# Third buffers for a transform's input and its two halves, and the last software DMAs moved to other queues

## The chip, the cores and the metric

One core of one Trainium2 chip runs the whole program. The metric is the device time in microseconds (us) of one execution. The engines are TensorE (PE, with its weight loads as PEld), VectorE (DVE), ScalarE (ACT), GpSimd (POOL) and SyncE (SP). SP, ACT and POOL also issue DMA transfers; each of these engines takes its instructions and its DMA issues strictly in order, so that an issue that waits holds up everything behind it on that engine.

## The reference

```python
# x: (8, 3072, 256); weights come as float64
X = np.fft.rfft(x, axis=1)
x = np.fft.irfft(X * (filt_r + 1j * filt_i), n=3072, axis=1)      # per channel
x_prev = shift x by one position
xk = mu_k * x + (1 - mu_k) * x_prev
xr = mu_r * x + (1 - mu_r) * x_prev
k = max(xk @ w_k, 0)                                              # 256 -> 1024
x = sigmoid(xr @ w_r) * (k * k @ w_v)                             # 1024 -> 256
h = max(x @ w1, x @ w2, x @ w3)                                   # 256 -> 768
out = h @ w_out                                                   # 768 -> 256
```

## The kernel before

**The transform.** 3072 = 48 x 64, and each batch is transformed by matmuls in two stages. The a-stage (16 steps) loads `xa`, splits it into a rounded high part `xah` and the remainder `xal`, multiplies by the resident table `wa_s` into `pa`, copies that to `ao` and stores it to DRAM (`s1`). The b-stage (12 steps) loads a 512 KB table `wbc`, a filter `filt` and `xb`, splits `xb`, multiplies (`pb`), applies the filter on DVE and POOL, splits the result into `yh` and `yl`, multiplies back (`pc`), copies to `co` and stores to DRAM (`s2`). A product of two values costs three matmuls (`mm3`): high x high, high x low, low x high.

**The rest.** `y_load` brings 384 KB of `s2` into `cin`, `y_mm` finishes the inverse transform (`py`), mixes with the previous position (`xm`) and splits (`xh`, `xl`). `kv(i)` (64 chunks of 384 positions) does the three products with w_k, w_v, w_r (`pk`, `pv`, `pr`). `combos` and `second(p)` do the 768-wide layers for a pair of chunks, in nine blocks of seven products (`pb`, `pa`, `pe`) with combined weights streamed from DRAM into the `ws` tiles; `o_mm` does the last product.

**Weights.** They arrive as float64. `narrow` makes float32 of a piece: one ACT operation into `we` (L212), five DVE operations (L213, L214, L215 on `we`, L218, L219 on `wm`) and one POOL addition into `wf` (L222); the parts are then a copy on ACT (L229) or DVE (L231) and a subtraction on POOL (L232). Pieces 0 to 8 (w_k, w_v, w_r) run beside the transform of the first batch; the twelve others (nine of w1, w2, w3 and three of w_out) are put among the units of the first chunks.

**Buffers.** The pool `fp` has two buffers for each tag, unless a line says otherwise. Tag `fin` holds `xa`, `xb` and `wm`; tags `flo` and `fhi` hold `xal`, `xbl`, `yl` and `xah`, `xbh`, `yh` and, in turn, `wf`; tag `fo` holds `we`, `ao` and `co`.

**What sets the order.** The first batch's transform (`fft_first`) is plain float32 and has its order on SP, ACT and PE written by hand; its filter step on DVE is L547, and its product `q` on POOL is L544. Everything else is ordered by a scheduler with a timing model of its own, which sees the units in the order of the list `units`; the transform of batch b + 1 is interleaved with the units of batch b by `drive`, except that nothing of it stands in the first `lead` units of batch 0.

**Software DMAs.** Three kinds of transfer are issued by POOL and go by the software queue: `wa_s` (which casts on the way), the four stores `wvd` of the prepared w_v (L273), and, in the second batch's transform only, the twelve `wbc` tables (L367, casting), each of which ACT then stores to DRAM (`wbcd`, L369) for the later batches to read.

Of the kernel before, what the change touches and what calls it, by code (L numbers as in the profile page):

```python
# [94 lines left out]
def as_float(bits):  # L95
    return float(np.uint32(bits).view(np.float32))
# [29 lines left out]
def tile_spectral_moe(ctx: ExitStack, tc, x, filt, ones, wa, wa1, wi, wbc, wb1, wc1, filt1, filt0, mu, w_k, w_v, w_r, w1, w2, w3, w_out, out):  # L126
    nc = tc.nc
    B = x.shape[0]
    P = 128
    C = 256  # L130
# [33 lines left out]


    wa_s = cpool.tile([NP, 2, NQ], F32R, name="wa_s")
    nc.gpsimd.dma_start(wa_s, wa)
    wi_s = cpool.tile([NQ, 2, NP], F32, name="wi_s")
    mu_s = cpool.tile([P, 2, 2], F32, name="mu_s")
    nmu_s = cpool.tile([P, 2, 2], F32, name="nmu_s")  # L170

    def load_small():
        nc.scalar.dma_start(wi_s, wi)
        nc.scalar.dma_start(mu_s, mu)
        nc.vector.tensor_scalar(nmu_s, mu_s, -1.0, 1.0, op0=ALU.mult, op1=ALU.add)

# [5 lines left out]
    cnt = [0]  # L182

    def piece(src, kt, t0, t1, c0, c1, parts):

        wide = src.dtype != F32
        if wide:
            src = src.bitcast(I32)
        v = src.rearrange("(t p) n -> p t n", p=P)
        a, c = t1 - t0, c1 - c0  # L190
        st = {}

        def load(stage=None):
            if stage is not None:
                st["t"] = stage.rearrange("p (a n) -> p a n", a=a)
            elif wide:
                st["t"] = fp.tile([P, a, 2 * c], I32, tag="filt", name="wst", bufs=3)
            else:
                st["t"] = fp.tile([P, a, c], F32, tag="filt", name="wst", bufs=3)
            k = 2 if wide else 1  # L200
            nc.sync.dma_start(st["t"], v[:, t0:t1, k * c0 : k * c1])

        def narrow(late=True):
            if not wide:
                st["r"] = st["t"]
                return
            w = st["t"].rearrange("p a (n k) -> p a n k", k=2)
            low, high = w[:, :, :, 0], w[:, :, :, 1]

            e = fp.tile([P, a, c], I32, tag="fo", name="we")  # L210
            ef = e.bitcast(F32)
            nc.scalar.activation(ef, high.bitcast(F32), AF.Abs)  # L212
            nc.vector.tensor_scalar(ef, ef, as_float(0x38000000), as_float(0x47EFFFFF), op0=ALU.max, op1=ALU.min)  # L213
            nc.vector.tensor_scalar(e, e, 3, 0x3FFFFFFF, op0=ALU.logical_shift_left, op1=ALU.bitwise_and)  # L214
            nc.vector.scalar_tensor_tensor(e, high, -0x40000000, e, ALU.bitwise_and, ALU.bitwise_or)  # L215
            m = fp.tile([P, a, c], I32, tag="fin", name="wm")
            mf = m.bitcast(F32)
            nc.vector.tensor_scalar(m, e, -0x800000, None, op0=ALU.bitwise_and)  # L218
            nc.vector.scalar_tensor_tensor(mf, low.bitcast(U32), 2.0**-52, mf, ALU.mult, ALU.mult)  # L219
            cnt[0] += 1  # L220
            r = fp.tile([P, a, c], F32, tag=("flo", "fhi")[cnt[0] % 2], name="wf")
            nc.gpsimd.tensor_tensor(r, ef, mf, ALU.add)  # L222
            st["r"] = r

        return load, narrow, lambda late=True: parts(st["r"], late)

    def to_parts(hi, lo, r, late):
# [23 lines left out]
    wv_d = [dp.tile([P, 2, 2, C], F32, tag=f"wvd{q}", name=f"wvd{q}", bufs=1) for q in range(NF // 2)]  # L251
# [17 lines left out]
    def wv_job(q):  # L269
        def parts(r, late):  # L270
            t = fp.tile([P, 2, 2, C], F32R, tag="wbc", name="wvs", bufs=3)
            to_parts(t[:, :, 0], t[:, :, 1], r, late)
            nc.gpsimd.dma_start(wv_d[q], t.bitcast(F32))  # L273

        return piece(w_v, NF, 2 * q, 2 * q + 2, 0, C, parts)

# [45 lines left out]
    wjobs2 = pipelined([wu_job(k) for k in range(NB)] + wo[2])  # L322


    s2_of = {}
    wbc_d = {}

    def fft(b):

# [5 lines left out]
        pieces = []  # L335

        def a_load(s):
            t = fp.tile([NP, 2, C], F32, tag="fin", name="xa")
            nc.sync.dma_start(t, xv[:, 2 * s : 2 * s + 2, :])
            hi = fp.tile([NP, 2, C], F32R, tag="fhi", name="xah")  # L340
            lo = fp.tile([NP, 2, C], F32R, tag="flo", name="xal")
            split(hi, lo, t, nc.gpsimd)
            st["a", s] = hi, lo

# [17 lines left out]

        def b_load(s):
            w = fp.tile([NK, 4, 2, NK], F32R, tag="wbc", name="wbc", bufs=3)
            if b == 1:

                nc.gpsimd.dma_start(w, wbc[:, s])  # L367
                wbc_d[s] = dp.tile([NK, 4, 2, NK], F32, tag=f"wbcd{s}", name=f"wbcd{s}", bufs=1)
                nc.scalar.dma_start(wbc_d[s], w.bitcast(F32))  # L369
            else:  # L370
                nc.sync.dma_start(w.bitcast(F32), wbc_d[s])
            f = fp.tile([NK, 2, 2, C], F32, tag="filt", name="filt", bufs=3)
            nc.sync.dma_start(f, filt[:, s])
            t = fp.tile([NK, 2, C], F32, tag="fin", name="xb")
            nc.sync.dma_start(t, s1.rearrange("m r g c -> (m r) g c")[:, 2 * s : 2 * s + 2, :])
            hi = fp.tile([NK, 2, C], F32R, tag="fhi", name="xbh")
            lo = fp.tile([NK, 2, C], F32R, tag="flo", name="xbl")
            split(hi, lo, t)
            st["b", s] = w, f, hi, lo

        def b_mm(s):
            w, f, hi, lo = st.pop(("b", s))
            p = ps.tile([NK, 2, C], F32, tag="pm", name="pb")
            for g in range(2):
                mm3(p[:, g], [(w[:, 0, g], w[:, 1, g])], [(hi[:, g], lo[:, g])], g > 0, True)

            fr, fi = f[:, 0], f[:, 1]
            H = NK // 2
            nc.vector.scalar_tensor_tensor(fi[:H], p[H:], -1.0, fi[:H], ALU.mult, ALU.mult)
            nc.vector.tensor_tensor(fi[H:], p[:H], fi[H:], ALU.mult)  # L390
            nc.vector.tensor_tensor(fr, p, fr, ALU.mult)
            (nc.gpsimd).tensor_tensor(fr, fr, fi, ALU.add)
            yh = fp.tile([NK, 2, C], F32R, tag="fhi", name="yh")
            yl = fp.tile([NK, 2, C], F32R, tag="flo", name="yl")
            split(yh, yl, fr)
            st["c", s] = w, yh, yl

# [477 lines left out]
    units = kv(0) + kv(1) + kv(2) + [(0.0, lambda: combos(0))] + kv(3)  # L875
    marks, cuts = {}, {}
    before2 = len(units)
    s, left = second(0)
    units += s
    units.append((0.0, lambda: combos(1)))  # L880
    for p in range(1, NPAIR):
# [5 lines left out]
        s, left = second(p)  # L887
# [11 lines left out]

    for k, fn in enumerate(wjobs2):  # L900
        units.insert(min(3 + int(k * (before2 - 3) / (NB + 1.5)), before2 + 10 + 3 * (k - NB)) + k, (0.0, fn))
    n2 = len(wjobs2)

    lead = before2 + n2
    starts = [0] + [marks[b] + n2 for b in range(1, B)]
# [62 lines left out]
```

## Time and profile before

| | |
|---|---|
| median of 3 runs | 3200.22 us (3198.54 to 3203.57) |
| the profiled execution | 3198.21 us, span 3196.4 us |
| mean granted clock of TensorE | 0.991 |
| busy: PE, ACT, POOL, DVE | 97%, 60%, 58%, 56% |
| DMA | 676.38 MB moved, of which 8.46 MB by the software queue |

A busy share is a mean over the whole span. With PE at 97% the question is where the other 3% stand and what PE waits for there, so the stretches are read one by one: the start up to 120 us, the conversion of the weights up to the first `second` at about 225 us, the second batch's transform, and the long steady part behind 480 us.

### The profile page before, as it was taken

What the parts mean: (1) busy time and instruction counts of PE and PEld (TensorE: products, weight loads), DVE (VectorE), ACT (ScalarE), POOL (GpSimd) and SP (SyncE); (2) the same over time, 40 slices, a digit from 0 to 9 for tenths busy, and PEclk for the clock granted to TensorE, in tenths of its full rate; (3) what the DMA queues carried; (4) which work ended last, traced back from release to release, by engine and by line L of the source; (5) the groups of instructions that cost most, each with busy time, mean ns of one, the idle gap of its engine ahead of it and who ended that gap; (6) DMA issues with size and microseconds to landing.
All of it is one profiled execution on the core that took longest, in us unless ns stands there. A gap on an engine that the chain in (4) does not pass through costs nothing.

```text
span 3196.4 us, 55749 instructions
## 1 busy us (share of the span) xinstructions
PE 3105.7 (97%) x19256; PEld 3031.7 (95%) x19256; DVE 1784.9 (56%) x2882; ACT 1913.8 (60%) x4024; POOL 1864.1 (58%) x1619
## 2 busy tenths in 40 slices
PE   6799999999999999999999999999999999999998
PEld 4789999999999999999999999999999999999998
DVE  4865564456554665456645466446664456555554
ACT  5556556656666566656666566665666566655554
POOL 3545675567655676546666566566665567544443
PEclk9899999999999999999999999999999999999999
DMA  8767796657766676757766577665876667555553
GB/s 292 234 227 226 235 329 192 195 181 247 246 197 184 213 241 211 215 173 234 257 198 186 178 259 252 198 191 165 269 249 189 190 195 245 182 170 160 166 168 122
DMA packets 397783, 676.38 MB, mean 212 GB/s; under 512 B 41920, under 2 KB 153664, under 8 KB 396864
## 3 DMA queue, kind: packets, MB, share of 16 engines
q1 hardware_dynamic: 328336, 585.61, 58.4%
q10 hardware_dynamic: 66752, 78.75, 7.2%
q0 software_dynamic: 2416, 8.46, 0.8%
q8 instruction: 156, 2.56, 0.3%
q14 instruction: 123, 1.01, 0.1%
HBM read 580.51 MB, written 92.14 MB: 210 GB/s over the span
## 4 chain that ended last, share of the span: by engine, by line
PE 84%; DMA 6%; DVE 5%; issue 2%; ACT 2%; POOL 1%; ACTq 0%; SPq 0%; POOLq 0%; DVEq 0%
PE pb L153 19%; PE pk L153 14%; PE pv L153 14%; PE po L153 12%; PE pe L153 9%; PE pa L153 7%; PE pr L153 4%; PE py L153 3%; DMA ws<-wud 3%; PE pc L153 2%; DVE xm L607 1%; DMA xb<-s 1%; PE ps L153 1%; DVE sc L665 1%; DVE m L748 1%
## 5 line engine op out<-in xcount | busy, mean ns | idle before, releaser
L153 PE MATMUL pb<-x,ws 128*128 128x384 f32 x3456 | 753.1, 338 | 23.0 <-DMA ws<-wud 16.9
L179 POOL TENSOR_TENSOR hh<-m,hh 128x384 fp32r<-128x384 f32 x384 | 402.2, 1056 | 522.4 <-ACT hh L178 426.3
L179 POOL TENSOR_TENSOR klo<-kr,khi 128x384 fp32r<-128x384 f32 x492 | 515.8, 1058 | 231.6 <-ACT khi L178 218.7
L153 PEld LDWEIGHTS pb<-x,ws 128*128 128x128 f32 x3456 | 598.7, 188 | 39.0 <-issue 15.2
L633 DVE SCALAR_TENSOR_TENSOR kr<-pk,kr 128x384 f32<-128x384 f32 x512 | 280.7, 553 | 444.9 <-ACT kr L632 443.6
L153 PE MATMUL po<-wo_hi,hh 128*128 128x256 f32 x2304 | 481.0, 283 | 3.1 <-ACT hh L178 1.6
L153 PE MATMUL pv<-khi,ws 128*128 128x384 f32 x2048 | 474.6, 337 | 4.0 <-ACT khi L178 4.0
L153 PEld LDWEIGHTS po<-wo_hi,hh 128*128 128x128 f32 x2304 | 389.9, 190 | 7.6 <-ACT hh L178 4.0
L153 PE MATMUL pe<-x,ws 128*128 128x384 f32 x1728 | 389.0, 337 | 0.6
L178 ACT CAST khi<-kr 128x384 fp32r<-128x384 f32 x512 | 260.2, 513 | 185.0 <-DVE kr L633 167.6
L153 PEld LDWEIGHTS pv<-khi,ws 128*128 128x128 f32 x2048 | 360.4, 188 | 7.0 <-ACT khi L178 5.3
L153 PE MATMUL pk<-xh,wk_hi 128*128 128x384 f32 x1024 | 341.4, 338 | 7.6 <-ACT xh L178 6.2
L153 PE MATMUL pk<-xl,wk_hi 128*128 128x384 f32 x1024 | 343.6, 336 | 0.9 <-DVE xl L179 0.9
L153 PE MATMUL pk<-xh,wk_lo 128*128 128x384 f32 x1024 | 343.4, 335 | 0.0
L153 PE MATMUL po<-wo_lo,hh 128*128 128x256 f32 x1152 | 316.6, 282 | 0.0
L632 ACT ACTIVATE kr<-pk 128x384 f32<-128x384 f32 x512 | 249.9, 490 | 109.0 <-POOL klo L179 48.7
L748 DVE TENSOR_TENSOR m<-sc,m 128x384 f32<-128x384 f32 x384 | 307.8, 806 | 9.2
L153 PEld LDWEIGHTS pe<-x,ws 128*128 128x128 f32 x1728 | 296.0, 188 | 3.1 <-PE pb L153 2.2
L153 PE MATMUL pv<-klo,ws 128*128 128x384 f32 x1024 | 292.3, 337 | 0.8 <-POOL klo L179 0.4
L179 POOL TENSOR_TENSOR xl<-xm,xh 128x768 fp32r<-128x768 f32 x126 | 233.4, 1869 | 89.7 <-ACT xh L178 89.7
L178 ACT CAST hh<-m 128x384 fp32r<-128x384 f32 x384 | 193.0, 514 | 134.2 <-DVE m L748 67.0
L607 DVE SCALAR_TENSOR_TENSOR xm<-yt,nmu_s,xm 128x384 f32<-128x384 f32 x256 | 180.1, 748 | 145.4 <-ACT xm L606 145.4
(129 smaller groups left out, 6028.0 us busy)
## 6 DMA issues: line engine op xcount, KB each, us to landing
ws<-wud SPq DMA_DIRECT2D x864, 256.0 KB, 3.5
ws<-wvd SPq DMA_DIRECT2D x512, 256.0 KB, 3.3
filt<-in_filt SPq DMA_DIRECT2D x84, 512.0 KB, 5.3
ws<-wud SPq DMA_DIRECT2D x288, 128.0 KB, 3.5
wbc<-wbcd SPq DMA_DIRECT2D x72, 512.0 KB, 5.4
cin<-s SPq DMA_DIRECT2D x64, 384.0 KB, 4.2
out_dram<-osb ACTq DMA_DIRECT2D x192, 128.0 KB, 3.1
xb<-s SPq DMA_DIRECT2D x85, 256.0 KB, 3.5
```

The costliest lines, as they stand in the source:

```text
L153: nc.tensor.matmul(o, lhsT=wgt, rhs=rhs, start=start, stop=stop, skip_group_check=more)
L178: nc.scalar.copy(hi, src)
L179: (lo_eng or nc.gpsimd).tensor_tensor(lo, src, hi.bitcast(F32), ALU.subtract)
L607: nc.vector.scalar_tensor_tensor(v[:, h], yt[:, h, :, :MC], nmu_s[:, w, h : h + 1], v[:, h], ALU.mult, ALU.add)
L632: nc.scalar.activation(r, p, AF.Relu)
L633: nc.vector.scalar_tensor_tensor(r, p, 0.0, r, ALU.max, ALU.mult)
L665: eng.tensor_tensor(t, a, b, ALU.subtract)
L748: nc.vector.tensor_tensor(m, c, m, ALU.max)
```

## The change

- Tags `fin`, `flo` and `fhi` get a third buffer, in room taken from the software queue's scratch (4096 to 1024).
- `wa_s` is loaded by ACT's queue into a float32 tile of tag `fin` and copied by DVE.
- The four `wvd` stores are issued by ACT.
- The `wbc` tables are rounded ahead of the second batch's transform, in 24 units `short(s, n)` of half a table each: SP loads 256 KB into `wbf` (tag `fin`), ACT copies it into `wbr` (tag `fo`, which keeps two buffers), SP stores it to `wbcd`. The units stand at places 24, 28, ... 116 of the list, inside the lead. The second batch then reads its twelve tables from `wbcd` on SP, as the later ones do.

```diff
     wa_s = cpool.tile([NP, 2, NQ], F32R, name="wa_s")
-    nc.gpsimd.dma_start(wa_s, wa)
...
     def load_small():
         nc.scalar.dma_start(wi_s, wi)
+        t = fp.tile([NP, 2, NQ], F32, tag="fin", name="wa_t", bufs=3)
+        nc.scalar.dma_start(t, wa)
+        nc.vector.tensor_copy(wa_s, t)
...
-            m = fp.tile([P, a, c], I32, tag="fin", name="wm")
+            m = fp.tile([P, a, c], I32, tag="fin", name="wm", bufs=3)
...
-            r = fp.tile([P, a, c], F32, tag=("flo", "fhi")[cnt[0] % 2], name="wf")
+            r = fp.tile([P, a, c], F32, tag=("flo", "fhi")[cnt[0] % 2], name="wf", bufs=3)
...
-            nc.gpsimd.dma_start(wv_d[q], t.bitcast(F32))
+            nc.scalar.dma_start(wv_d[q], t.bitcast(F32))
...
-    wbc_d = {}
+    wbc_d = [dp.tile([NK, 4, 2, NK], F32, tag=f"wbcd{s}", name=f"wbcd{s}", bufs=1) for s in range(NG // 2)]
+
+    def short(s, n):
+        t = fp.tile([NK, 2, 2, NK], F32, tag="fin", name="wbf", bufs=3)
+        tc.keep_in_program_order(nc.sync.dma_start(t, wbc[:, s, n : n + 2]))
+        r = fp.tile([NK, 2, 2, NK], F32R, tag="fo", name="wbr")
+        nc.scalar.copy(r, t)
+        nc.sync.dma_start(wbc_d[s][:, n : n + 2], r.bitcast(F32))
...
-            t = fp.tile([NP, 2, C], F32, tag="fin", name="xa")
+            t = fp.tile([NP, 2, C], F32, tag="fin", name="xa", bufs=3)
...
-            hi = fp.tile([NP, 2, C], F32R, tag="fhi", name="xah")
-            lo = fp.tile([NP, 2, C], F32R, tag="flo", name="xal")
+            hi = fp.tile([NP, 2, C], F32R, tag="fhi", name="xah", bufs=3)
+            lo = fp.tile([NP, 2, C], F32R, tag="flo", name="xal", bufs=3)
...
-            if b == 1:
-
-                nc.gpsimd.dma_start(w, wbc[:, s])
-                wbc_d[s] = dp.tile([NK, 4, 2, NK], F32, tag=f"wbcd{s}", name=f"wbcd{s}", bufs=1)
-                nc.scalar.dma_start(wbc_d[s], w.bitcast(F32))
-            else:
-                nc.sync.dma_start(w.bitcast(F32), wbc_d[s])
+            nc.sync.dma_start(w.bitcast(F32), wbc_d[s])
...
     for k, fn in enumerate(wjobs2):
         units.insert(min(3 + int(k * (before2 - 3) / (NB + 1.5)), before2 + 10 + 3 * (k - NB)) + k, (0.0, fn))
-    n2 = len(wjobs2)
+    for k in range(NG):
+        units.insert(24 + 4 * k, (0.0, lambda k=k: short(k // 2, k % 2 * 2)))
+    n2 = len(wjobs2) + NG
...
-    nc = _bacc.Bacc("TRN2", target_bir_lowering=False, num_devices=1, dynamic_dma_scratch_size=4096)
+    nc = _bacc.Bacc("TRN2", target_bir_lowering=False, num_devices=1, dynamic_dma_scratch_size=1024)
```

`xb`, `xbh`, `xbl`, `yh` and `yl` get `bufs=3` in the same way. The changed kernel's own line numbers are a few higher: L550 there is L547 here, L213 to L222 become L215 to L224, and L178 becomes L180.

Where the change moves instructions, the compiled orders show it. The first place is DVE at the end of the first batch's transform. A number behind a name counts tiles; L547 (L550 after the change) is the filter step of the transform, the other rows convert pieces 6 and 7 of the weights. Before, the last L547 stood here:

```order
L215 SCALAR_TENSOR_TENSOR we_625<-wst_471,we_625 128x512 [waits DMAHW3_49,DVE_49]
L547 SCALAR_TENSOR_TENSOR filt1_418<-pb_509,sgn_119,filt1_418 128x512 [waits DMAHW1_49,PE_49,Pool_49]
L218 TENSOR_SCALAR wm_630<-we_625 128x512 [waits DVE_49]
L219 SCALAR_TENSOR_TENSOR wm_630<-wst_471,wm_630 128x512 [waits DVE_49]
L213 TENSOR_SCALAR we_639<-we_639 128x512 [waits Activation_49,Pool_49]
L214 TENSOR_SCALAR we_639<-we_639 128x512 [waits DVE_49]
L215 SCALAR_TENSOR_TENSOR we_639<-wst_507,we_639 128x512 [waits DMAHW4_49,DVE_49]
L213 TENSOR_SCALAR we_653<-we_653 128x512 [waits Activation_49,Pool_49]
L218 TENSOR_SCALAR wm_644<-we_639 128x512 [waits DVE_49]
L214 TENSOR_SCALAR we_653<-we_653 128x512 [waits DVE_49]
L219 SCALAR_TENSOR_TENSOR wm_644<-wst_507,wm_644 128x512 [waits DVE_49]
L215 SCALAR_TENSOR_TENSOR we_653<-wst_568,we_653 128x512 [waits DMAHW7_49,DVE_49]
```

In the changed kernel the same place on DVE reads:

```order
L550 SCALAR_TENSOR_TENSOR filt1_377<-pb_487,sgn_130,filt1_377 128x512 [waits PE_49,Pool_49]
L216 TENSOR_SCALAR we_653<-we_653 128x512 [waits DVE_49]
L215 TENSOR_SCALAR we_667<-we_667 128x512 [waits Activation_49]
L217 SCALAR_TENSOR_TENSOR we_653<-wst_521,we_653 128x512 [waits DMAHW5_49,DVE_49]
L216 TENSOR_SCALAR we_667<-we_667 128x512 [waits DVE_49]
L220 TENSOR_SCALAR wm_658<-we_653 128x512 [waits DVE_49]
L217 SCALAR_TENSOR_TENSOR we_667<-wst_582,we_667 128x512 [waits DMAHW0_49,DVE_49]
L550 SCALAR_TENSOR_TENSOR filt1_408<-pb_504,sgn_130,filt1_408 128x512 [waits PE_49,Pool_49]
L221 SCALAR_TENSOR_TENSOR wm_658<-wst_521,wm_658 128x512 [waits DVE_49]
L220 TENSOR_SCALAR wm_672<-we_667 128x512 [waits DVE_49]
L550 SCALAR_TENSOR_TENSOR filt1_432<-pb_523,sgn_130,filt1_432 128x512 [waits DMAHW2_49,PE_49,Pool_49]
L221 SCALAR_TENSOR_TENSOR wm_672<-wst_582,wm_672 128x512 [waits DVE_49]
```

Of the twelve conversion operations that stood behind the transform's last filter step (ten are L213 to L219 of the last two pieces, two belong to the piece ahead), one still stands behind it; the other eleven have moved ahead of it.

The second place is ACT where the first two blocks of `second` end and the second batch's a-stage begins. In the changed kernel ACT has the following there (`v` is the last copy that the first two blocks need; `wbr` the copies of `short`; `we` and `wo_hi` belong to the last weights; `xah` is the first high part of the second batch):

```order
L704 COPY v_2168<-pb1_2129 128x384 [waits PE_49]
L231 CAST wo_hi_90<-wf_1892 128x512 [waits Pool_49]
L334 CAST wbr_1920<-wbf_1918 128x512 [waits DMAHW5_49,DVE_49]
L334 CAST wbr_1955<-wbf_1953 128x512 [waits DMAHW6_49,DMAHW1_49,Activation_49]
L334 CAST wbr_1996<-wbf_1994 128x512 [waits DMAHW3_49,DMAHW2_49,Activation_49]
L214 ACTIVATE we_2009<-wst_1882 128x512 [waits DMAHW4_49,Activation_49]
L334 CAST wbr_2053<-wbf_2051 128x512 [waits DMAHW6_49,DMAHW5_49,Activation_49]
L334 CAST wbr_2076<-wbf_2074 128x512 [waits DMAHW7_49,Pool_49]
L231 CAST wo_hi_90<-wf_2017 128x512
L334 CAST wbr_2101<-wbf_2099 128x512 [waits DMAHW2_49,DMAHW1_49,Activation_49]
L214 ACTIVATE we_2104<-wst_2007 128x512 [waits DMAHW3_49,Activation_49]
L180 CAST xah_2123<-xa_2121 96x512 [waits DMAHW5_49]
```

Before, none of the `wbr` copies existed, and `xah` stood among the copies of the last chunk ahead of `second`. SP carries the stores of these copies and the load of `xa` in the same queue, in this order after the change:

```order
L335 DMA wbcd9_101<-wbr_1920 128x512 [waits DMAHW3_49,Activation_49]
L335 DMA wbcd9_101<-wbr_1955 128x512 [waits DMAHW4_49,Activation_49]
L335 DMA wbcd10_102<-wbr_1996 128x512 [waits DMAHW5_49,Activation_49]
L332 DMA wbf_2051<-in_wbc 128x512 [waits DMAHW6_49]
L332 DMA wbf_2074<-in_wbc 128x512 [waits DMAHW7_49,DMAHW2_49]
L376 DMA filt_3604<-in_filt 128x1024 [waits DMAHW0_49,DVE_49,Activation_49]
L335 DMA wbcd10_102<-wbr_2053 128x512 [waits DMAHW1_49,Activation_49]
L332 DMA wbf_2099<-in_wbc 128x512 [waits DMAHW6_49]
L335 DMA wbcd11_103<-wbr_2076 128x512 [waits DMAHW3_49,Activation_49]
L335 DMA wbcd11_103<-wbr_2101 128x512 [waits DMAHW4_49,Activation_49]
L348 DMA xa_2121<-in_x 96x512 [waits DMAHW7_49,DMAHW5_49]
```

The first load of the second batch's input stands behind the last of the 24 stores; before, the three first loads of `xa` stood between two `ws` loads of the last chunk. The third place is PE in the same stretch, where the product that needs `xah` has moved. Before (`pb`, `pa1` and `pe` are products of the blocks, `pa` of the transform; 1950 and 1995 are the first two blocks, 2054 is the third):

```order
L153 MATMUL pe1_2003<-x2_1672,ws_1880 128x384 [waits DMAHW1_49,DVE_49]
L153 MATMUL pe1_2003<-x2_1672,ws_1880 128x384 x2
L153 MATMUL pa_2042<-xah_1989,wa_s_69 96x512 [waits DMASW0_49,DVE_49]
L153 MATMUL pa_2042<-xal_1990,wa_s_69 96x512
L153 MATMUL pa_2042<-xah_1989,wa_s_69 96x512
L153 MATMUL pb1_2054<-x2_1654,ws_1940 128x384 [waits DMAHW5_49,DVE_49]
```

In the changed kernel the first two blocks are 2079 and 2129, and the third is 2188:

```order
L153 MATMUL pb1_2129<-x2_1763,ws_2043 128x384 [waits Activation_49]
L153 MATMUL pb1_2129<-x2_1763,ws_2043 128x384 x2
L153 MATMUL pe1_2137<-x2_1772,ws_2056 128x384 [waits DVE_49]
L153 MATMUL pe1_2137<-x2_1772,ws_2056 128x384 x2
L153 MATMUL pb1_2129<-x2_1769,ws_2131 128x384 [waits DMAHW4_49,Activation_49]
L153 MATMUL pb1_2129<-x2_1769,ws_2131 128x384 x2
L153 MATMUL pa_2176<-xah_2123,wa_s_69 96x512 [waits PE_49,Activation_49]
L153 MATMUL pb1_2188<-x2_1748,ws_2064 128x384 [waits DMAHW3_49]
```

PE now has twelve of the fourteen products of the first two blocks ahead of the wait for `xah` (five before), and the third block behind it.

## Rows read from the trace of the kernel before

**Rows 1.** The page, first part: busy us (share of span) xinstructions.

```profile
PE 3105.7 (97%) x19256; PEld 3031.7 (95%) x19256; DVE 1784.9 (56%) x2882; ACT 1913.8 (60%) x4024; POOL 1864.1 (58%) x1619
```

**Rows 2.** Windows: us; busy PE, PEld, DVE, ACT, POOL; clock; DMA share; GB/s.

```profile
0.00:84.00 84.00, 58.97 (x179) 36.92 (x180) 38.14 (x54) 41.41 (x66) 34.15 (x33) 0.90 0.86 284
84.00:120.00 36.00, 17.93 (x85) 16.53 (x84) 34.13 (x54) 17.36 (x36) 16.77 (x15) 0.67 0.88 277
120.00:200.00 80.00, 78.72 (x531) 77.87 (x530) 66.26 (x103) 49.04 (x99) 39.60 (x30) 1.00 0.62 200
200.00:240.00 40.00, 33.80 (x206) 32.12 (x206) 14.26 (x24) 19.64 (x43) 14.86 (x15) 0.99 0.76 262
240.00:320.00 80.00, 76.95 (x457) 73.32 (x457) 44.66 (x62) 49.70 (x106) 47.59 (x40) 0.98 0.73 226
400.00:480.00 80.00, 75.42 (x470) 73.30 (x469) 55.59 (x82) 47.62 (x102) 57.49 (x52) 0.98 0.94 327
480.00:3196.00 2716.00, 2685.32 (x16828) 2644.56 (x16826) 1484.12 (x2427) 1641.75 (x3481) 1598.97 (x1388) 1.00 0.65 204
```

**Rows 3.** Timeline around 100 us: start, us, engine, instruction, idle before with releaser.

```profile
80.92 0.74 DVE L547 SCALAR_TENSOR_TENSOR filt<-pb,sgn,filt 128x512 f32<-128x512 f32 x1
...
85.14 0.98 DVE L213 TENSOR_SCALAR we<-we 128x512 f32<-128x512 f32 x1 [2.01 <-ACT we L212]
...
92.04 0.69 DVE L219 SCALAR_TENSOR_TENSOR wm<-wst,wm 128x512 f32<-128x512 uint32 x1
...
98.10 3.70 PE L153 MATMUL py<-wi_s,cin 96*128 96x96 f32 x16 [12.18 <-DMA eye<-in_ones]
...
103.34 2.14 ACT L606 ACTIVATE xm<-yt,mu_s 128x384 f32<-128x384 f32 x4
...
105.71 3.21 DVE L607 SCALAR_TENSOR_TENSOR xm<-yt,nmu_s,xm 128x384 f32<-128x384 f32 x4
```

**Rows 4.** Timeline around the first block of `second`.

```profile
204.99 0.62 ACT L178 CAST xah<-xa 96x512 fp32r<-96x512 f32 x1 [2.90 <-DMA xa<-in_x]
...
225.35 2.03 PE L153 MATMUL pb<-x,ws 128*128 128x384 f32 x9
...
228.26 0.40 PE L153 MATMUL pa<-xah,wa_s 96*96 96x512 f32 x1
```

**Rows 5.** DMA issues, 130 to 330 us: queue, count, KB, us to landing.

```profile
ws<-wud SPq DMA_DIRECT2D x47, 256.0 KB, 3.9
...
xa<-in_x SPq DMA_DIRECT2D x16, 192.0 KB, 4.1
```

**Rows 6.** DMA issues, whole span, the same columns.

```profile
out_dram<-osb ACTq DMA_DIRECT2D x192, 128.0 KB, 3.1
...
s<-co ACTq DMA_DIRECT2D x84, 256.0 KB, 5.3
```

**Rows 7.** Windows behind idle stretches of PE, columns as in rows 2.

```profile
106.00:108.00 2.00, 1.08 (x3) 1.08 (x4) 2.00 (x3) 0.61 (x2) 1.45 (x1) 0.50 0.94 190
...
241.00:243.00 2.00, 2.00 (x7) 1.85 (x7) 0.49 (x1) 0.48 (x1) 0.00 (x0) 0.50 1.03 399
```

**Rows 8.** Timeline at the two gaps beside software DMAs.

```profile
238.65 0.34 ACTq L369 DMA_DIRECT2D wbcd<-wbc  x1
239.03 0.48 ACT L701 COPY v<-pb 128x384 f32<-128x384 f32 x1 [1.14 <-DMA s<-ao]
239.56 2.29 PE L153 MATMUL pb<-x,ws 128*128 128x384 f32 x6 [3.58 <-ACT v L701]
...
400.25 0.58 POOL L367 DMA_DIRECT2D wbc<-in_wbc  x1 [0.38 <-PE pc L153]
400.69 4.80 DVE L665 TENSOR_TENSOR sc<-sc,gate 128x384 f32<-128x384 f32 x1
...
409.63 0.36 PE L153 MATMUL pc<-yh,wbc 128*128 128x256 f32 x1 [3.77 <-DVE filt L391]
```

**Rows 9.** PE's waits from 480 us on: waited for, us in total, times, longest.

```profile
PE pb L153 <- DMA ws<-wud: 14.6, 15, 2.0
```

More of the change, by code (lines that the diff above doesn't have):

```diff
@@ L364, in b_load @@
             w = fp.tile([NK, 4, 2, NK], F32R, tag="wbc", name="wbc", bufs=3)
-            if b == 1:
-                nc.gpsimd.dma_start(w, wbc[:, s])
-                wbc_d[s] = dp.tile([NK, 4, 2, NK], F32, tag=f"wbcd{s}", name=f"wbcd{s}", bufs=1)
-                nc.scalar.dma_start(wbc_d[s], w.bitcast(F32))
-            else:
-                nc.sync.dma_start(w.bitcast(F32), wbc_d[s])
+            nc.sync.dma_start(w.bitcast(F32), wbc_d[s])
             f = fp.tile([NK, 2, 2, C], F32, tag="filt", name="filt", bufs=3)
             nc.sync.dma_start(f, filt[:, s])
-            t = fp.tile([NK, 2, C], F32, tag="fin", name="xb")
+            t = fp.tile([NK, 2, C], F32, tag="fin", name="xb", bufs=3)
             nc.sync.dma_start(t, s1.rearrange("m r g c -> (m r) g c")[:, 2 * s : 2 * s + 2, :])
-            hi = fp.tile([NK, 2, C], F32R, tag="fhi", name="xbh")
-            lo = fp.tile([NK, 2, C], F32R, tag="flo", name="xbl")
+            hi = fp.tile([NK, 2, C], F32R, tag="fhi", name="xbh", bufs=3)
+            lo = fp.tile([NK, 2, C], F32R, tag="flo", name="xbl", bufs=3)
             split(hi, lo, t)
@@ L392, in b_mm @@
             (nc.gpsimd).tensor_tensor(fr, fr, fi, ALU.add)
-            yh = fp.tile([NK, 2, C], F32R, tag="fhi", name="yh")
-            yl = fp.tile([NK, 2, C], F32R, tag="flo", name="yl")
+            yh = fp.tile([NK, 2, C], F32R, tag="fhi", name="yh", bufs=3)
+            yl = fp.tile([NK, 2, C], F32R, tag="flo", name="yl", bufs=3)
             split(yh, yl, fr)
```

## The prediction

> **What bounds the kernel now.** I read the busy shares first: PE 3105.7 us of a span of 3196.4 [rows 1]. So 90.7 us are left in which PE has nothing, and only a change in those, or new ones beside them, can move the time; the profiled execution takes 1.8 us more than its span (3198.21). The windows by stage say where they are [rows 2]: 25.0 us before 84 (84.00 − 58.97), 18.1 from 84 to 120, 1.3 from 120 to 200, 6.2 to 240, 3.0 to 320, 4.6 from 400 to 480 and 30.7 in the 2716 us behind 480. The kernel is thus bound by PE after 120 us, and by loads, DVE and GpSimd before. The transfers that the change takes off the software queue lie before 84 (`wvd`) and between about 230 and 480 (`wbc`). Next I read what ended PE's waits behind 480: 14.6 us of the 30.7 are waits for a streamed weight, `ws`, 15 of them, the longest 2.0 [rows 9]. Then the timelines of the start, of the first `second` and of two gaps beside software DMAs [rows 3, 4, 8]. A difference of under 0.2%, 6.4 us, is about what a measurement of this kernel cannot tell from none.
>
> **The start: +6.5.** Before, DVE's last filter step of the first transform begins at 80.92, ends 0.74 later at 81.66, and everything behind it (last `pc`, its copy and store, the load of `cin`) leads to `py` at 98.10, PE having waited 12.18 [rows 3]. The order shown above moves eleven conversion operations ahead of that step. They run from 81.66 to about 91.9 in the trace of before, the last conversion operation (92.04) being the one that stays behind; 2.01 of that is DVE waiting for ACT [rows 3]. So 10.3 us with that idle, 8.3 without it, go ahead of the filter step, on an engine that had no work to spare there. The first thing behind `py` that DVE must do is `xm` at 105.71; ACT's first of the four pieces of 2.14 that began at 103.34 was ready about 103.9 (103.34 + 2.14/4), so 1.8 of the shift is slack, because DVE was then held by later conversions which the change has done before. 8.3 − 1.8 = 6.5. Ends: 10.3, if the idle stays and no slack is got back; −1.8, if all eleven find idle time earlier on DVE (it is busy 38.14 of the first 84 us [rows 2]). I take 6.5, since the operations ahead of 81.66 that I could see stand close behind each other. The `wa_s` load and its DVE copy are one transfer and one operation at a time when PE has not yet begun with `pa`, worth nothing; the four `wvd` issues leave POOL and stand on ACT ahead of the last store of the transform, four times 0.34 (the ACT issue in [rows 8]), part of the upper end.
>
> **The drain ahead of the third block: +21.** This is the large term. In the changed order ACT has, behind the last copy `v` that PE's first two blocks need, `wo_hi`, six `wbr` copies and two `we`, and only then `xah`; PE has twelve products and then `pa`, which needs `xah`, ahead of the third block. Tag `fo` has two buffers. Of the eight tiles every other one takes the same buffer: 1920, 1996, 2053, 2101. Each copy must wait until the store of the one before has been issued and has landed. A copy is 0.62 (the `xah` copy has the same size but for the rows [rows 4]); an issue about 0.35 [rows 8]; the landing I take from the 256 KB transfers of that stretch, 3.9 [rows 5]. One turn is 0.62 + 0.35 + 3.9 = 4.87. From the end of `v`: `wo_hi` 0.62, copy 1920 0.62, three turns 14.6, the issue of the last store and of `xa` 0.7, landing of `xa` 4.1 [rows 5], `xah` 0.62: 21.3. PE still has one product behind `v`, three matmuls, about 0.7 (2.03/9 × 3, [rows 4]). So PE stands for about 21 us, with the whole remaining program queued behind it. Nothing hides it: PE's third block needs no `xah`, but stands behind it in order. Before, `xa` was loaded and `xah` made at 204.99, and `pa` ran at 228.26, 2.9 after the first block began at 225.35 with no wait [rows 4]. Ends by the landing: 3.1 (the shortest store of a similar kind) gives 18.4, 5.3 (the 256 KB store of the b-stage) gives 25 [rows 6]. A further low end is 12, if the scheduler's lag is partly made up: if the first three copies find their stores landed before `v`.
>
> **Cold clock: +2.** Behind the 3.58 us gap at 239.56 the granted clock was 0.50, the lower of its two levels, from 241 to 243; after the long wait at 98 it was still 0.50 at 106 to 108 [rows 7]. At that level two us of matmuls lose one. Behind a stall of 21 us I count 2, ends 1 and 4.
>
> **The 24 copies elsewhere: +2.** Seventeen of the 24 copies, 17 × 0.62 = 10.5 us of ACT, stand before the drain, most of them from 120 to 200, where ACT is busy 49.0 of 80 and PE 78.7 [rows 2]. Their cover is ACT's 31 us of idle time. If each stood in front of a `khi` that PE waits for, the loss would be the whole 10.5; if none, nothing. PE now waits only 1.3 us there, so I take 2.
>
> **Gains: −8.1.** Two gaps of PE go with the software DMAs [rows 8]. At 239.56 PE waits 3.58 us for `v`; ACT had stood at the store `wbcd` (issued 238.65) until its software load had landed, and that store disappears: −3.58 and −1.7 for the slow clock behind it (about 3.4 us at half speed, rows 7 showing two of them), −5.3. At 409.63 PE waits 3.77 for the filter; DVE's operation of 4.80 us began at 400.69, right behind POOL's `wbc` issue at 400.25 of 0.58. What ties the two together is nearness in time alone, so half counts: 3.77 and 1.8 for the slow clock are 5.6, half is −2.8. Ends: 0 and −10.9. The Trainium skill ("SBUF — State Buffer", section "SBUF: two separate sides") says that DVE and GpSimd share a port pair which one of them holds for a whole instruction, and that software DMAs, whose descriptors GpSimd writes, starve under DVE while those of ACT's or SP's queue don't; by it the whole 5.6 would go, and the sum be 2.8 lower. No row here shows a starved descriptor.
>
> **The steady part: −2.** From the second batch on, PE's order is nearly that of before. Third buffers let `xa` and `xb` loads leave SP earlier, and `ws` loads behind them too; at best all 14.6 us [rows 9] go. At worst they grow by as much again, since SP now also waits for slots of stores and loads it didn't carry. I take −2, near nothing, because the longest of those waits is 2.0 and the other causes (`filt`, `cin`) stay.
>
> **Sum.** 6.5 + 21 + 2 + 2 − 8.1 − 2 = 21.4; on the profiled execution 3198.2 + 21.4 = 3219.6. The median of the runs lies 2.0 above that execution, so 3221.6, which I give as 3222.
>
> **The rivals.**
> 1. *Both delays are there, but smaller*: the start finds idle time (0 to 3), the drain is 12, the gains come whole (−10.9): 3200.2 + 3 + 12 + 2 + 1 − 11 = 3207, with 3204 to 3211 around it. For it: the scheduler gave that order by its own timing, and the chip may have the copies done earlier.
> 2. *It does nothing*: the queues that were changed are off the path. Seventeen POOL issues of 0.58 [rows 8] are 9.9 us on an engine busy 58% [rows 1], and the two gaps come back elsewhere as the order around them is reshuffled: 3200, 3194 to 3206. Against it: the drain stands in the order itself. The Trainium skill ("DMA: Bandwidth & Descriptors", section "Issuing engines are not separate DMA queues") says that transfers run on the same 16 engines whoever issues them, and that another issuing engine saves only the time of the issue; by it alone the result is this rival. The trace has the DMA share at 0.94 from 400 to 480 [rows 2], which agrees that moving transfers frees no engine of theirs.
> 3. *Faster*: the drain is hidden, because the 24 copies keep up. The place is the same; it decides when the last seven stores have landed before `v` of the second block, that is, when ACT has at most one `wbr` left there. Then −5.3 − 5.6 for the gaps, −8 of the 14.6 of `ws`, +6.5 at the start: −12.4, 3188, with 3184 to 3194. For it: third buffers loosen three tags; against it: `fo`, the tag that the copies go through, keeps two.
>
> **How the numbers follow.** The likeliest, both delays as priced: 0.60, 3211 to 3237 (the start by −1.5 or +4, the drain by −3 or +4, copies up to +8, the gaps by −3 or +8, taken not all at once). Rival 1: 0.15. Rival 2: 0.11. Rival 3: 0.14. Rival 1 is slower by over 0.2% in about two thirds of its range, 0.10, same in 0.05; rival 2 is the same in nearly all. Faster 0.14, same 0.14, slower 0.72. The range that leaves out at most 2 in 10: rival 3 (0.14) falls below 3196, and about 0.05 of the likeliest lies over 3242, so 3196 to 3242.
>
> **What would show it.** In the new trace: one idle stretch of PE of 18 to 25 us, 8 us behind the first block of `second`, ended by ACT `xah`, and ahead of it ACT waiting three times for stores of `wbr`; `py` at about 106 instead of 98.1, DVE's last filter step at about 90; no gap of 3.6 us about 14 us behind the first block. The prediction is wrong if `xah` stands ready when PE reaches it, or if the copies of ACT are found among the `khi` with PE waiting at each.

## The result, and the profile after

The changed kernel takes 3230.95 us in the median of four runs (3228.21 to 3236.75), the kernel before 3200.84: a ratio of 1.0095, 95% interval 1.0079 to 1.0111. It is slower, as forecast; +30.1 us where +21.4 was forecast. The profiled execution is the slowest of the four, 3236.75 us, 38.5 above that of before (3198.21). So its rows sum to some 6 us more than the median: what the rows account for is 38.5, 8.4 more than the +30.1 of the medians. The differences between kernels below are read as ratios.

First the page's line of busy times:

```profile
PE 3112.4 (96%) x19256; PEld 3041.4 (94%) x19256; DVE 1787.6 (55%) x2883; ACT 1921.5 (59%) x4048; POOL 1858.8 (57%) x1602
```

PE is idle 122.5 us of the span of 3234.9, against 90.7. The windows by stage, with the columns of [rows 2], say where:

```profile
0.00:84.00 84.00, 54.80 (x156) 34.22 (x156) 35.60 (x54) 39.16 (x62) 30.19 (x29) 0.80 0.86 281
84.00:120.00 36.00, 14.86 (x57) 12.59 (x57) 25.84 (x34) 12.79 (x26) 16.17 (x12) 0.69 0.82 256
...
240.00:320.00 80.00, 51.61 (x302) 47.60 (x301) 33.15 (x54) 41.17 (x85) 35.03 (x29) 0.83 0.81 260
...
518.50:3234.90 2716.40, 2688.55 (x16840) 2650.61 (x16838) 1488.83 (x2429) 1638.60 (x3483) 1602.45 (x1388) 1.00 0.65 203
```

PE's idle time from 240 to 320 is 28.4 us, against 3.0 in [rows 2]. The last row is the stretch of 2716.4 us that ends with the program, so that it can stand beside the same stretch of before:

```profile
480.00:3196.40 2716.40, 2685.32 (x16828) 2644.56 (x16826) 1484.12 (x2427) 1641.75 (x3481) 1598.97 (x1388) 1.00 0.65 204
```

There PE is idle 27.9 us instead of 31.1: the late part has gained 3.2. What PE waited for up to 480 (us in total, times, longest):

```profile
PE pa L153 <- ACT xah L180: 26.0, 1, 26.0
...
PE pc L153 <- ACT wcr L465: 8.7, 1, 8.7
PE pc L153 <- DVE filt L550: 7.8, 5, 3.3
```

Before, there was no wait for the table copies `wcr`, and the filter steps held PE longer:

```profile
PE pc L153 <- DVE filt L547: 10.6, 7, 3.2
```

**The stall before the third block** is one wait of 26.0 us. Its timeline, PE first, then ACT, then SP (start, us, instruction, idle before it; a row can merge several instructions):

```profile
242.90 1.21 PE L153 MATMUL pb<-x,ws 128*128 128x384 f32 x6
...
251.65 0.69 PE L153 MATMUL pb<-x,ws 128*128 128x384 f32 x3
278.37 0.74 PE L153 MATMUL pa<-xah,wa_s 96*96 96x512 f32 x1 [26.04 <-ACT xah L180]
```

```profile
250.61 0.48 ACT L704 COPY v<-pb 128x384 f32<-128x384 f32 x1
253.40 0.62 ACT L231 CAST wo_hi<-wf 128x512 fp32r<-128x512 f32 x1 [2.31 <-POOL wf L224]
258.55 1.31 ACT L334 CAST wbr<-wbf 128x512 fp32r<-128x512 f32 x2 [4.54 <-DMA wbf<-in_wbc]
262.88 0.62 ACT L334 CAST wbr<-wbf 128x512 fp32r<-128x512 f32 x1 [3.02 <-DMA wbcd<-wbr]
263.49 0.66 ACT L214 ACTIVATE we<-wst 128x512 f32<-128x512 f32 x1
267.41 0.62 ACT L334 CAST wbr<-wbf 128x512 fp32r<-128x512 f32 x1 [3.26 <-DMA wbf<-in_wbc]
...
273.46 0.62 ACT L334 CAST wbr<-wbf 128x512 fp32r<-128x512 f32 x1 [3.96 <-DMA wbf<-in_wbc]
...
277.70 1.14 ACT L180 CAST xah<-xa 96x512 fp32r<-96x512 f32 x2 [2.97 <-DMA xa<-in_x]
```

```profile
252.29 1.59 SPq L332 DMA_DIRECT2D wbf<-in_wbc  x2
...
259.19 4.65 SPq L335 DMA_DIRECT2D wbcd<-wbr  x3
263.90 0.92 SPq L332 DMA_DIRECT2D wbf<-in_wbc  x2
...
268.42 0.43 SPq L332 DMA_DIRECT2D wbf<-in_wbc  x1
269.00 5.43 SPq L335 DMA_DIRECT2D wbcd<-wbr  x2
274.53 0.85 SPq L348 DMA_DIRECT2D xa<-in_x  x2
```

Read from `v` at 250.61 to 251.09: one wait for a weight's addition, one of 4.54 for a load of `wbf` that SP issued only from 252.29 on, then three turns up to 274.08, then `xa`, issued behind the last store. Two of the three turns were ended by a load, which stood on SP behind the stores that waited for ACT's copies. In all that time PE stands at the product that needs `xah`; the third block comes behind it.

**The start** is late too. On ACT at the end of the first transform (the store of w_v is at L275, the table copies at L465):

```profile
67.66 1.25 ACT L214 ACTIVATE we<-stage 128x512 f32<-128x512 f32 x2 [0.46 <-ACT e L477]
74.29 0.67 ACT L214 ACTIVATE we<-wst 128x512 f32<-128x512 f32 x1 [5.37 <-POOL wf L224]
77.09 0.33 ACTq L275 DMA_DIRECT2D wvd<-wvs  x1
77.45 1.04 ACT L465 COPY wcr<-wcr 64x1024 f32<-64x1024 f32 x1 [2.50 <-POOL wvs L234]
```

and on DVE and PE behind it:

```profile
90.81 0.74 DVE L550 SCALAR_TENSOR_TENSOR filt<-pb,sgn,filt 128x512 f32<-128x512 f32 x1
...
78.55 1.22 PE L153 MATMUL pc<-filt,wcr 128*128 128x256 f32 x2 [8.73 <-ACT wcr L465]
...
110.95 3.70 PE L153 MATMUL py<-wi_s,cin 96*128 96x96 f32 x16 [14.13 <-DMA cprev<-s]
118.78 1.65 PE L153 MATMUL pk<-xh,wk_hi 128*128 128x384 f32 x4 [3.27 <-ACT xh L180]
```

`py` starts 12.85 us later than the 98.10 of [rows 3], and the first `pk` at 118.78 instead of 106.92, 11.9 later. The account of the profiled executions: 11.9 to the first `pk`; `second` begins at 242.90 instead of 225.35 [rows 4], 17.6 later, so 5.7 more in the first chunks; then 26.0; together 43.6. The end is 38.5 later, so 5.1 came back.

### The profile page after: what moved, and what is told of

Its sections match the earlier page's. It is cut to its first block, busy times and chain, and to the rows that moved or that the text cites. A ratio compares the mean times of both kernels' runs of the same rounds, so it can differ in the third digit from the quotient of the medians.

```text
span 3234.9 us, 55906 instructions
## 1 busy us (share of the span) xinstructions
PE 3112.4 (96%) x19256; PEld 3041.4 (94%) x19256; DVE 1787.6 (55%) x2883; ACT 1921.5 (59%) x4048; POOL 1858.8 (57%) x1602
## 4 chain that ended last, share of the span: by engine, by line
PE 82%; DMA 6%; DVE 4%; ACT 1%; issue 1%; POOL 0%; SPq 0%; ACTq 0%; POOLq 0%; DVEq 0%
PE pb L153 18%; PE pk L153 14%; PE pv L153 13%; PE po L153 12%; PE pe L153 9%; PE pa L153 6%; PE pr L153 4%; DMA ws<-wud 4%; PE py L153 3%; PE pc L153 2%; DVE sc L668 1%; DMA wbf<-in_wbc 1%; DMA xb<-s 1%; DVE x L181 1%; DVE kr L636 0%
## 5 line engine op out<-in xcount | busy, mean ns | idle before, releaser
L153 PEld LDWEIGHTS pb<-x,ws 128*128 128x128 f32 x3456 | 599.7, 189 | 33.7 <-ACT u L704 10.6
L180 ACT CAST khi<-kr 128x384 fp32r<-128x384 f32 x512 | 260.3, 513 | 204.6 <-DVE kr L636 189.7
L153 PEld LDWEIGHTS pv<-khi,ws 128*128 128x128 f32 x2048 | 361.0, 189 | 11.1 <-ACT khi L180 10.2
L180 ACT CAST hh<-m 128x384 fp32r<-128x384 f32 x384 | 193.5, 515 | 128.7 <-DVE m L751 65.7
```

What stands on the lines that cost most here:

```text
L153: nc.tensor.matmul(o, lhsT=wgt, rhs=rhs, start=start, stop=stop, skip_group_check=more)
L180: nc.scalar.copy(hi, src)
```

## The experiments

Edits are against the changed kernel if nothing else is said. A ratio is that to the kernel before, run on the same chip.

**The first w_v store, later (wvd_late).**

```diff
-            nc.scalar.dma_start(wv_d[q], t.bitcast(F32))
+            store = lambda: nc.scalar.dma_start(wv_d[q], t.bitcast(F32))
+            held.append(store) if q == 0 else store()
...
             if s == 8:
                 w_double(2)
+        held.pop()()
```

> The changed kernel, with the first of the four w_v stores issued by ACT after the transform's last copies instead of in the middle of them. Theory A (ACT stands in its hand-written order at that store, waiting for GpSimd, about 8.7 us with the copies of the transform's tables and of v behind it): py begins near 99 to 101 instead of 110.95, the 8.73 us wait of PE for the table copy is gone, and the time falls by 9 to 12, to about 3219 to 3222. Theory B (the prediction's: the conversion operations ahead of the last filter step on DVE make the start late, the issue costs only 0.34): py stays near 110 and the time within 2 of the changed kernel's. Neither touches the 26 us stall before the third block.

3222.61 us, 1.0074 (1.0059 to 1.0088). The start is back, as PE's timeline of this run shows:

```profile
98.50 3.70 PE L153 MATMUL py<-wi_s,cin 96*128 96x96 f32 x16 [11.63 <-DMA ws<-wvd]
```

The wait for `xah` is 26.0 us again. Theory A: 12.45 us of the 12.85 at `py` go back to the place of one store whose issue takes 0.33. In ACT's hand-written order it stood ahead of the table copies, and waited for GpSimd's half of the same weight. With the store elsewhere the scheduler also put the conversions back behind DVE's last filter step, which begins where it began before:

```profile
80.51 0.74 DVE L553 SCALAR_TENSOR_TENSOR filt<-pb,sgn,filt 128x512 f32<-128x512 f32 x1
```

So the prediction's cause, the conversions ahead of that step, was itself an effect of the store's place, and no run has one without the other. That it isn't what made PE late is read from the waits above: the one that is new is for the table copies. The ratio fell by 0.0021, some 7 us; 9 to 12 were expected, and the two intervals are too wide to tell 7 from 12. In the profiled executions `second` begins 14.0 us sooner than in the changed kernel (228.92), and the span is 13.3 shorter.

**All four w_v stores back on GpSimd (wvd_pool).**

```diff
-            nc.scalar.dma_start(wv_d[q], t.bitcast(F32))
+            nc.gpsimd.dma_start(wv_d[q], t.bitcast(F32))
```

> The changed kernel with the four w_v stores back on GpSimd's queue, nothing else. If the store's place in ACT's hand-written order is the whole of the late start: py at 97 to 100, no wait for the table copies, the time 8 to 13 below the changed kernel, like the run with the late store. If the reordered conversions on DVE count for themselves: py at 103 or later.

1.0051 (1.0033 to 1.0069; 3221.37 beside 3203.84), which is 0.0044 or 14 us under the changed kernel's ratio. In the timeline of this run `py` is where it was before:

```profile
99.31 3.70 PE L153 MATMUL py<-wi_s,cin 96*128 96x96 f32 x16 [13.39 <-DMA eye<-in_ones]
```

DVE's last filter step is back too (80.93), so the second theory wasn't tested alone here either. The start hangs on the queue of these stores. The Trainium skill ("DMA: Bandwidth & Descriptors", section "Issuing engines are not separate DMA queues") says that another issuing engine saves only the time of the issue. For the transfers themselves no run here speaks against it; for the kernel the engine that issues decided 12 us, by what stands behind the issue in that engine's order.

**The transform interleaved 40 units later (lead40).**

```diff
-    lead = before2 + n2
+    lead = before2 + n2 + 40
```

> The changed kernel with the second batch's transform interleaved from 40 units later on, nothing else changed. Theory A (the 26 us stall is PE standing, in order, at the first product of the transform while the third block could run): the stall goes, PE waits for single copies instead, 3 to 8 us in all, and the time falls by 18 to 25, to 3206 to 3213. Theory B (the six table copies on ACT hold the blocks' own copies too, so the stall is only broken up): the waits of PE from 240 to 320 still sum to 20 or more and the time falls by under 8.

3230.01 us, with a spread of 3224.43 to 3239.25; 1.0095 (1.0078 to 1.0113), as the changed kernel. The stall was broken up: PE's longest waits of this run from 240 to 320 are

```profile
PE pa L153 <- ACT xah L180: 6.2, 1, 6.2
PE po L153 <- ACT wo_hi L231: 4.3, 1, 4.3
```

and its window there:

```profile
240.00:320.00 80.00, 65.28 (x367) 59.55 (x366) 43.55 (x68) 46.36 (x95) 40.91 (x34) 0.89 0.86 280
```

14.7 us idle instead of 28.4 there, and the profiled execution is 9 us shorter, yet the median of the runs is not. Neither theory holds as stated. Of the 13.7 gained there, 3.3 came back in the last 2716.4 us (31.1 of idle time, in the changed kernel 27.9); why, no run shows.

**A third buffer for fo (fo3).**

```diff
-            e = fp.tile([P, a, c], I32, tag="fo", name="we")
+            e = fp.tile([P, a, c], I32, tag="fo", name="we", bufs=3)
...
-        r = fp.tile([NK, 2, 2, NK], F32R, tag="fo", name="wbr")
+        r = fp.tile([NK, 2, 2, NK], F32R, tag="fo", name="wbr", bufs=3)
```

(`ao` and `co` in the same way; the software scratch goes to 512.)

> The changed kernel with a third buffer for tag fo (we, ao, co and the table copies wbr). Theory A (the turns of the last copies are copy, store issue and store landing through two buffers, the prediction's): three turns become two, the stall falls from 26 to 14 to 20 and the time by 6 to 12. Theory B (the loads of wbf, behind ws loads and the stores in SP's queue, set the turns; in the changed kernel ACT's waits there name them four times): the stall stays at 22 to 27, the time within 4 of the changed kernel's.

3233.54 us, 1.0105 (1.009 to 1.0121): no gain in time. The stall is shorter by 4.7 (21.3). `py` begins at 116.4, 5 later than in the changed kernel, but `second` at 242.20, 0.7 sooner. From there on most of the 4.7 comes back as other waits, as the windows below show.

**The tables' stores on ACT (store_act), and both edits (store_act_fo3).**

```diff
-        nc.sync.dma_start(wbc_d[s][:, n : n + 2], r.bitcast(F32))
+        nc.scalar.dma_start(wbc_d[s][:, n : n + 2], r.bitcast(F32))
```

> The changed kernel with the 24 stores of the staged tables issued by ACT behind their own copies, and so out of SP's queue, where they stood ahead of the next load of wbf. Theory A (the turn of the last copies is set by SP's order: load, copy, store issue, then only the next load): loads run ahead of the copies, the stall at xah falls from 26 to 12 to 18 and the time by 8 to 14. Theory B (the prediction's: copy, issue and landing of the store through two fo buffers): three turns of 0.62 + 0.35 + 3.5 to 3.9 are left, the stall stays at 18 to 24 and the time falls by 2 to 8, only as the first load is no longer late.

> The run before this one with the third buffer of fo as well. If SP's order and the two fo buffers are two limits side by side, each about as long as the other, then neither edit alone takes much of the stall and both together do: the stall at xah falls to 4 to 12 and the time by 14 to 22 against the changed kernel. If it still stands over 18, something else sets it (the loads' own time, or conversions).

1.0081 (1.0063 to 1.0098) and 1.005 (1.0032 to 1.0067). PE's wait for `xah` with the third buffer of fo alone:

```profile
PE pa L153 <- ACT xah L180: 21.3, 1, 21.3
```

With the stores on ACT alone:

```profile
PE pa L153 <- ACT xah L180: 23.2, 1, 23.2
```

With both, where a wait for `v` stands beside it:

```profile
PE pa L153 <- ACT xah L180: 8.6, 1, 8.6
PE pb L153 <- ACT v L704: 6.2, 1, 6.2
```

26.0 with neither, 21.3 and 23.2 with one, 8.6 with both, beside 6.2 at another place. With the stores on ACT alone, ACT's timeline names the landing of stores, as the prediction had it (4.58 in the longest):

```profile
261.64 0.62 ACT L334 CAST wbr<-wbf 128x512 fp32r<-128x512 f32 x1 [4.58 <-DMA wbcd<-wbr]
```

There only the first and the last of these copies wait over 1 us for a load (4.15 and 3.39). With the third buffer alone the copies' named waits are for loads (the longest 3.75), with one of 3.01 for a store, ahead of a `we`. The wait for `xah` isn't the whole loss, so here are the 80 us from the first block of `second` on: the third buffer alone, the stores on ACT alone, then both:

```profile
242.20:322.20 80.00, 53.56 (x304) 49.14 (x304) 34.63 (x58) 44.03 (x90) 39.07 (x33) 0.83 0.81 259
```

```profile
242.92:322.92 80.00, 52.30 (x296) 47.82 (x296) 33.55 (x56) 42.89 (x86) 37.00 (x31) 0.83 0.79 248
```

```profile
238.60:318.60 80.00, 61.41 (x337) 56.93 (x337) 36.45 (x59) 45.96 (x94) 42.26 (x36) 0.85 0.84 268
```

PE is idle 28.4 us there in the changed kernel, 26.4 and 27.7 with one edit, 18.6 with both, and 4.4 in the kernel before. Two limits of nearly one length stood side by side: two buffers that wait for stores, and loads that wait in SP's order behind those stores. Taking either away shows the other, and taking both away brings 9.8 us of the 24.0 that the changed kernel loses there, less than the wait for `xah` alone suggests; the loads' own time and the weights' conversions are left.

**The tables staged in the a-stage (spread), and with the late store (spread_late).**

```diff
-    for k in range(NG):
-        units.insert(24 + 4 * k, (0.0, lambda k=k: short(k // 2, k % 2 * 2)))
...
                 if s >= 1:
                     a_mm(s - 1)
+                if b == 1 and s < NG // 2:
+                    short(s, 0)
+                    short(s, 2)
```

> The changed kernel with the 24 table units taken out of the lead: two stand in each of the first twelve a-stage steps of the second batch's transform. Theory A (the table units placed ahead of the first product that needs xah, through the two buffers of fo, make the stall and the longer chunk phase): no stall of over 5 us near the third block, second begins 4 to 6 us sooner after py than in the changed kernel, and the time falls by 22 to 30, to 3201 to 3209. Theory B (the copies cost the same wherever they stand, since they share fo with ao and ACT with the copies of the blocks): several waits on ao or xah in the a-stage that sum to over 15 us, and the time falls by under 10. The start (py at 110) stays.

> The run before this one, and in addition the first w_v store issued by ACT after the transform's last copies. If the start and the table units are two separate causes that add up: py near 98.5 as in the run with the late store alone, and 8 to 13 below the run with the table units spread: 3190 to 3200. If the gains beside the software loads that the prediction counted (-5.3 and -2.8) are real, it ends at or under the kernel before, 3190 to 3197; if they come back as other waits, 3198 to 3206.

3241.53 us, 1.0126 (1.0111 to 1.014), and 3232.82 us, 1.0093 (1.0079 to 1.0106). Theory A fell. The first `pa` no longer waits, but the next ones do, as PE's waits of the first of the two runs show:

```profile
PE pa L153 <- ACT xah L180: 26.8, 8, 8.8
```

The same loop of load, copy and store runs between the steps of the a-stage, whose `ao` shares `fo` and whose `xa` shares SP. It costs as much in eight waits as in one. The forecast for the second run (3190 to 3200) fell with it. The late store brings 0.0033, about 10.5 us, so the start adds up with the rest. What the 17 copies among the first chunks cost stays open. Without them `second` begins 118.8 us behind the first `pk` in the first of these runs (237.67 − 118.90) and 122.5 in the second (226.47 − 103.99); with them it is 124.1 in the changed kernel and 117.9 with the third buffer of `fo`, and 118.4 before.

**Third buffers alone (third_only), and none (two_bufs).** The first is the kernel before with `bufs=3` on the ten tiles of `fin`, `flo` and `fhi`, and the smaller software scratch; the second is the changed kernel without them.

> The kernel before with the third buffers and the smaller software scratch alone; all transfers go where they went before. Theory A (third buffers alone hardly touch what PE waits for; the gaps of 3.6 us and 3.8 us beside the software loads stay): 3197 to 3203. Theory B (third buffers let the transform's loads leave SP earlier and shorten the 14.6 us of ws waits): 3186 to 3195. Theory C (the reshuffled order by itself costs, and part of the 30 us is the buffers'): over 3206.

> The changed kernel without the third buffers (two for fin, flo and fhi), all transfers on their new queues. Theory A (the third buffers have no part in the 30 us; third buffers alone gave no difference): 3226 to 3238, stall at xah 24 to 30, py 109 to 113. Theory B (third buffers soften the queue moves, as wbf shares fin with xa and wm): over 3240, the stall over 32. Theory C (the scheduler's reshuffle from third buffers is the cause): under 3215.

The first 3202.26 us, 1.0006 (0.9998 to 1.0014): no difference. PE's waits for `v` and for the filter are there as before, from 120 to 480:

```profile
PE pb L153 <- ACT v L701: 4.1, 1, 4.1
PE pc L153 <- DVE filt L391: 3.0, 1, 3.0
```

The second 3247.96 us, 1.0139 (1.0121 to 1.0157): Theory B in the time, not in the stall (27.2). Its waits of `pb` for `ws` behind 480 are the longest of the kernels here: 20.1, 14.6 in [rows 9].

**Tables copied in the b-stage itself (inline_late), and that without third buffers (inline_two).** With the late store, and without the units:

```diff
-            nc.sync.dma_start(w.bitcast(F32), wbc_d[s])
+            if b == 1:
+                for n in (0, 2):
+                    t = fp.tile([NK, 2, 2, NK], F32, tag="fin", name="wbf", bufs=3)
+                    nc.sync.dma_start(t, wbc[:, s, n : n + 2])
+                    nc.scalar.copy(w[:, n : n + 2], t)
+                nc.scalar.dma_start(wbc_d[s], w.bitcast(F32))
+            else:
+                nc.sync.dma_start(w.bitcast(F32), wbc_d[s])
```

> No table units at all: the second batch's b-stage loads each half table as float32 by SP, ACT copies the halves into wbc, and ACT stores the table as before the change; the first w_v store is late as in the run above; no software DMA is left. Theory A (what hurt was staging through fo ahead of time, not taking the tables off GpSimd): py near 98.5, no stall, the gap of 3.6 us behind ACT's store is gone since the copy that the store waits for is ACT's own, 3190 to 3198. Theory B (24 copies of 0.62 us on ACT and loads in tag fin beside xb hold the b-stage): waits of pb and pc from 300 to 480 grow by 8 or more, 3204 to 3212.

> The fast version (tables copied by ACT in the b-stage itself, first w_v store late) without the third buffers. Theory A (third buffers are worth something only where the queues are moved: wbf shares fin with xa, xb and wm): 8 to 17 slower than with them, 3192 to 3201. Theory B (no part: third buffers alone gave no difference to the kernel before): 3181 to 3188.

3183.98 us, 0.9943 (0.9931 to 0.9955): 17 us faster than the kernel before, the fastest version here, and faster than either theory's range. With two buffers 3208.06 us, 1.0014 (1.0003 to 1.0025), slower by 23 and so by more than Theory A's 8 to 17. With three buffers the copies in the b-stage cost PE nothing that shows, and both gaps are gone; two windows of the fast version, then the second of them in the one with two buffers:

```profile
200.00:240.00 40.00, 39.97 (x248) 39.04 (x247) 15.75 (x28) 21.70 (x46) 11.51 (x10) 1.00 0.64 207
...
400.00:480.00 80.00, 78.55 (x519) 77.77 (x518) 52.65 (x83) 54.53 (x118) 57.26 (x49) 1.00 0.96 325
```

```profile
400.00:480.00 80.00, 69.33 (x417) 65.81 (x416) 48.73 (x74) 46.71 (x97) 50.65 (x42) 0.96 0.87 299
```

With two buffers PE waits for the transform's input, whose tag the table loads share:

```profile
PE pb L153 <- ACT xbh L180: 6.8, 4, 4.8
```

From 400 to 480 PE is idle 1.45 us with three buffers and 10.7 with two; 4.6 in [rows 2].

## Why the prediction came out as it did

The direction and the likeliest case were right, the sum 8.7 us short of the measured +30.1. By its steps:

- **The start, +6.5, was mis-sized, and its cause was named wrongly.** It measured 11.9. The last filter step came at 90.81, where the text said about 90: the order on DVE was read rightly. That this sign came true was luck all the same, since it isn't what made PE late. The prediction put the four w_v stores at their issue, four times 0.34, and did not ask what stands behind the first of them on ACT: the table copies, then the last six `v` copies. PE waited 8.73 for the table copies, no longer than before for the filter steps (7.8, before 10.6), and with the store elsewhere `py` was back at 98.5 and 99.3. The slack counted as 1.8 was 1.0 (12.85 at `py`, 11.9 at `pk`).
- **The drain, +21, was the right place and half of the mechanism; it measured 26.0.** The three turns took 14.9 (from the end of the first copy at 259.2 to 274.08), 14.6 were priced; that they lie so near is in part luck, since two of the three turns were ended by loads, which the price did not contain. What was missing is ahead of them: 2.31 for a weight's addition and 4.54 for the first load, late on SP. That the turn was set by stores through two buffers is half of it, as the four kernels with and without each limit show.
- **The cold clock, +2**, could not be separated from the rest. The windows of the changed kernel show the granted clock at 0.50 in the stall and 0.88 from 280 to 290, 1.2 us less than full speed in those ten:

```profile
260.00:270.00 10.00, 0.00 (x0) 0.00 (x0) 2.67 (x5) 3.03 (x5) 1.62 (x2) 0.50 0.66 201
...
280.00:290.00 10.00, 9.82 (x48) 8.83 (x48) 3.93 (x7) 7.20 (x15) 9.18 (x8) 0.88 0.85 255
```

- **The copies among the chunks, +2.** The stretch from the first `pk` to `second` grew by 5.7, inside the bounds of 0 to 10.5. That the copies did it is not shown: it is 118.8 and 122.5 us long in the two kernels without them, 117.9 in one with them.
- **The gains, −8.1 and −2.** In the changed kernel's waits from 285 to 480 neither the wait for `v` nor that for the filter is left, and in their place stand 3.1 for `kr` and 2.4 for a block's copy. The later steps together gave back 5.1, which already holds what the cold clock cost; the prediction counted 8.1 (10.1 less 2 for the clock). The steady part has its −2 well: the last 2716.4 us gained 3.2. In the fast version PE is idle 5.8 us from 200 to 480, against 15.2 before, so the gaps can go without coming back. Whether the software load made the gap at 409 is not shown. By the Trainium skill ("SBUF — State Buffer", section "SBUF: two separate sides") a software DMA waits for its descriptors while DVE runs an operation in a two-port mode, as a float32 copy within SBUF does; the operation of 4.80 us [rows 8] takes two tensors, for which that section names a lock only against a GpSimd operation that reads SBUF. So the page doesn't by itself give the whole 5.6 that the prediction took from it, and no row shows a starved descriptor. The same operation was long once in the fast version too, which has no software DMA:

```profile
494.57 3.47 DVE L672 TENSOR_TENSOR sc<-sc,gate 128x384 f32<-128x384 f32 x1
```

- **The rivals.** That the copies keep up and the result is faster fell. Its reason against, two buffers in `fo`, was one of two. That the queues are off the path fell with the 12 us of one store.

What stays open: what the 24 copies cost outside the drain, and where the whole gain of the fast version comes from. Its span is 16.8 us shorter than before. PE's idle time is 10.2 less: 2.3 more up to 200, 9.4 less from 200 to 480, 3.1 less behind 480. The other 6.6 are PE's busy time for the same 19256 matmuls (3099.1 instead of 3105.7), and no run shows what made it shorter.

## What to carry to other kernels

Price a DMA by what stands behind it in the order of its issuing engine, above all where that order is written by hand and the transfer waits for another engine: the issue here took 0.33 us, and `py` began 12 later for it. When work is staged ahead of time, follow each buffer and each queue that the staging passes, and look for a second limit of the same length before widening one. Buffers that bring nothing alone can be what another change needs: the third ones were worth nothing in the kernel before, 14 us in the changed one (1.0139 to 1.0095) and 23 in the fast one (1.0014 to 0.9943).

## What the runs showed that was not expected

Taking the tables off GpSimd costs little when ACT, which was busy 60%, copies them just where they are used, with third buffers for the input that shares their tag: 24 copies of 0.62 us, and a kernel 17 us faster. The same copies, staged through DRAM ahead of time, make PE wait 26 us at one place or 26.8 in eight.
